# Pooled attention and routed experts: another order of the first loads, weight halves split earlier, two first-layer chunks in one group

## The chip, the core and the metric

The kernel runs on one core of one Trainium2 chip. The core has TensorE (matmuls, results in PSUM), VectorE, ScalarE, GpSimd and SyncE, each with an instruction stream of its own that runs in order; they wait for each other by semaphores. In profile rows they are PE (PEld for its weight loads), DVE, ACT, POOL and SP. The metric is the device time of the program in microseconds (us); lower is better.

## What is computed

Attention over keys and values that are averaged in groups of 8, then a layer of 8 experts of which each row takes one.

```python
k_p = k.reshape(B, H, Sp, pool, D).mean(axis=3)      # B=8, H=8, S=576, D=64, pool=8
v_p = v.reshape(B, H, Sp, pool, D).mean(axis=3)
scores = scale * np.matmul(q, k_p.transpose(0, 1, 3, 2))
attn = softmax(scores); x = attn @ v_p               # x: 4608 rows of 512
...
logits = x @ w_gate; e_idx = np.argmax(logits, axis=1)
gate_w = probs[np.arange(N), e_idx]; eom = sigmoid(x @ w_output_gate)
h = np.maximum(x[mask] @ w1[e], 0.0)                 # 512 -> 1024
out[mask] = gate_w[mask, None] * eom[mask, e, None] * (h @ w2[e])
```

Matmuls of the experts run on two-part operands: each f32 number is split into a high part (a rounded copy made by ScalarE) and a low part (what is left, a VectorE subtraction), and three products are summed.

## The kernel before

The attention works on 36 tiles of 128 rows (`NT`), a batch being 4.5 tiles. One pass of the main loop, `i` with halves `a` = 0, 1 (four heads each), issues: the scores of tile `i` (`scores`), the transposes of the probabilities of tile `i - 2` (`transpose_p`), the row maxima of tile `i` on VectorE (`peak`), the products with the values of tile `i - 3` (`values`), the exponentials on ScalarE (`softmax`) and the division (`normalise`). Two small generators' queues are worked between these (`work`): the routing of each group of four tiles and the pooling of values.

The order within each engine is written out by hand. What belongs to a batch is put into a table `plan` by `at(step, function, ...)`, and the entries of step `i + a/2 - 1/2` are issued at the end of pass (`i`, `a`), in the order in which they were put in: the batches' loads first, then their pooling, then the rest. For batch `b` with `f` = 4.5 `b`: keys are loaded at step `f - 8.5`, values at `f - 5` (not before step 0), queries at `f - 4.5`. All of these go through SP's one queue. Keys are pooled by three rounds of additions, on VectorE for batch 0 (`ready_k`) and on GpSimd (`pool_k`) later, then copied by ScalarE into `kbd` (`scale_k`). Values are pooled on VectorE for batch 0 (`first_v`); later GpSimd does the first round (`halve_v`, steps `f - 3` and `f - 2.5`) and VectorE the rest (`pool_v`, in the work queue from `f - 2`). All values pass through one buffer `vt`, so a load waits until the batch before has been pooled. Then seven ScalarE copies place them (`place_v`), TensorE turns them and multiplies them with the gates (`turn_v`, `gate_v`).

Towards the end of attention the first expert's weights are loaded in stages (`stage_in`) and split in halves of 512 columns (`split_hi` on ScalarE, `split_lo` on VectorE), and the first 384 rows of expert 0 are gathered and turned (`turn_x`). After the last tile the string `TAIL` gives the order: `M` one chunk of the first layer (12 matmuls of 384 columns, `hidden_chunk`), `H` and `L` its high and low part, `W` units of the routing, `a` and `d` halves of w1, `A` and `D` pieces of w2, `R` and `T` tables, `Y` a chunk of the second layer. Then the experts' loop runs; there GpSimd (`body` at line 1319) hands out the rows' ids and scales, gathers the next job's and scatters the results.

## Time and profile before

| what | us |
|---|---|
| median of three runs | 605.59 |
| lowest and highest of them | 602.8 and 607.97 |
| the profiled execution | 603.94 |
| its span, first to last instruction | 602.1 |

The profiled execution is one of its own and stands 1.65 us below the median. Its span begins at the first instruction, and the times in the rows below count from there. Attention lasts to about 151 us, the first layer and the start of the second of expert 0's first rows to about 183 us, and the experts' loop from there to the end. A row of the timeline gives start, length, engine, line and operation, what is written and read, the number of instructions merged, and in brackets how long the engine had been idle and for whom.

### The profile page before, as it was taken

Reading aid. Unit: us, or ns where it says so; the run is one execution under the profiler, and the core shown is the slowest. Engines: PE = TensorE matmul, PEld = TensorE weight load, DVE = VectorE, ACT = ScalarE, POOL = GpSimd, SP = SyncE. Lnnn points to the kernel's source line nnn. Section 1 sums busy time; section 2 is a strip of 40 time slices with the busy share of each in tenths; the row PEclk is TensorE's granted clock in tenths of the full one; section 3 lists DMA queues with packets and bytes.
Section 4 is the critical chain, followed back from the end, with each engine's and each line's share of the span. In section 5 each row is a group of like instructions: output and inputs, shape, how many; then the busy total and the mean of one; then the engine's idle time right before and its main releaser. Section 6 shows DMA issues by size and latency. Waiting matters only on the chain.

```text
span 602.1 us, 11826 instructions
## 1 busy us (share of the span) xinstructions
PE 572.3 (95%) x3427; PEld 519.2 (86%) x3428; DVE 365.1 (61%) x892; ACT 257.8 (43%) x709; POOL 223.1 (37%) x331
## 2 busy tenths in 40 slices
PE   2999999999899999999999999999999999999996
PEld 2898898888888989898989898898988898989894
DVE  6789999988888625698575323664263842232323
ACT  2988998787435304266344120441141420302120
POOL 2858789642524322233234131231202421213131
PEclk9999999999999999999999999999999999999999
DMA  9856899966377433589666213463033212010111
GB/s 337 312 236 270 316 349 369 348 232 198 140 238 182 170 99 118 147 234 335 177 215 201 62 37 88 139 195 65 35 139 102 46 21 84 2 52 19 41 30 36
DMA packets 44684, 96.61 MB, mean 160 GB/s; under 512 B 5515, under 2 KB 28475, under 8 KB 41664
## 3 DMA queue, kind: packets, MB, share of 16 engines
q1 hardware_dynamic: 29328, 48.95, 25.3%
q10 hardware_dynamic: 7488, 27.27, 13.5%
q0 software_dynamic: 7792, 19.61, 9.3%
q14 instruction: 57, 0.47, 0.3%
q8 instruction: 19, 0.31, 0.2%
HBM read 76.36 MB, written 22.91 MB: 165 GB/s over the span
## 4 chain that ended last, share of the span: by engine, by line
PE 68%; issue 2%; DVEq 0%; DVE 0%; POOL 0%; POOLq 0%
PE p_h L1015 34%; PE p_y L996 33%; PE p_y L665 1%; POOL out L1328 0%; DVE rows L1186 0%; DVEq L1189 0%; PE p_y L1050 0%; DVE q_even L1212 0%; DVEq L779 0%; DVEq L780 0%; DVEq L1219 0%; DVEq L910 0%; DVEq L837 0%; DVEq L1211 0%; DVEq L860 0%
## 5 line engine op out<-in xcount | busy, mean ns | idle before, releaser
L1095 ACT ACTIVATE ht<-p_h 128x384 fp32r<-128x384 f32 (+1 forms) x104 | 46.9, 451 | 245.9 <-PE p_h L1015 243.7
L1015 PE MATMUL p_h<-xt,w1b 128*128 128x384 f32 (+1 forms) x736 | 115.5, 317 | 1.9 <-issue 1.3
L1015 PEld LDWEIGHTS p_h<-xt,w1b 128*128 128x128 f32 x736 | 114.4, 189 | 3.2 <-issue 2.8
L1328 POOL DMA_INDIRECT out<-rows,dst x41 | 43.1, 1051 | 199.8 <-DVE rows L1186 196.6
L1197 DVE SCALAR_TENSOR_TENSOR ht<-p_h,ht 128x384 fp32r<-128x384 f32 (+1 forms) x104 | 52.3, 504 | 98.4 <-ACT ht L1095 98.3
L996 PE MATMUL p_y<-w2b,ht 128*128 128x512 f32 x480 | 110.4, 390 | 0.0
L996 PEld LDWEIGHTS p_y<-w2b,ht 128*128 128x128 f32 x480 | 89.8, 188 | 18.4
L1015 PE MATMUL p_h<-xt,w1a 128*128 128x256 f32 (+1 forms) x640 | 93.7, 306 | 1.2 <-DVE q_even L1212 1.0
L1015 PEld LDWEIGHTS p_h<-xt,w1a 128*128 128x128 f32 x640 | 92.8, 190 | 2.3 <-DVE q_even L1212 1.2
L996 PE MATMUL p_y<-w2a,ht 128*128 128x512 f32 x408 | 94.2, 390 | 0.4 <-PE p_y L665 0.4
L996 PEld LDWEIGHTS p_y<-w2a,ht 128*128 128x128 f32 x408 | 76.2, 188 | 16.4 <-issue 0.9
L1186 DVE TENSOR_SCALAR rows<-p_y,sc 128x512 f32<-128x512 f32 x41 | 30.1, 741 | 85.9 <-PE p_y L996 71.5
L287 ACT ACTIVATE p<-p_h,m 128x72 f32<-128x72 f32 x288 | 69.9, 345 | 13.4 <-DVE m L281 13.0
L309 PE MATMUL p_y<-vbd,pT 128*128 128x162 f32 (+3 forms) x400 | 68.5, 320 | 3.8 <-DVE xg L332 2.6
L1305 POOL DMA_INDIRECT rows<-xs,src x51 | 56.0, 1099 | 24.9 <-POOL src L1301 13.4
L309 PEld LDWEIGHTS p_y<-vbd,pT 128*128 128x128 f32 (+1 forms) x400 | 54.2, 179 | 8.7 <-issue 2.5
L440 POOL DMA_INDIRECT xs<-xg,where x36 | 36.1, 1003 | 42.5 <-DVE grec L326 20.7
L201 POOL TENSOR_TENSOR kq<-kq 128x288 f32<-128x288 f32 (+1 forms) x63 | 40.8, 673 | 15.0 <-DMA kq<-kT 14.2
L275 PE MATMUL p_h<-kbd,q_even 128*128 128x144 f32 (+1 forms) x160 | 28.9, 308 | 11.6 <-DMA q_even<-qT 8.8
L332 DVE TENSOR_TENSOR xg<-p_y,grec 128x240 f32<-128x240 f32 x72 | 35.3, 490 | 1.3
L1150 DVE STREAM_TRANSPOSE turned<-rows 128x512 f32<-128x512 f32 x51 | 32.4, 686 | 4.0 <-DMA rows<-xs 2.2
L275 PEld LDWEIGHTS p_h<-kbd,q_even 128*128 128x128 f32 (+1 forms) x160 | 22.9, 191 | 13.7 <-issue 9.3
(170 smaller groups left out, 660.3 us busy)
## 6 DMA issues: line engine op xcount, KB each, us to landing
stage<-wst ACTq DMA_DIRECT2D x52, 512.0 KB, 4.7
rows<-v SPq DMA_DIRECT2D x8, 1280.0 KB, 6.3
kq<-kT SPq DMA_DIRECT2D x7, 1152.0 KB, 12.0
rows<-xs SPq DMA_DIRECT2D x36, 192.0 KB, 3.8
stage<-wst SPq DMA_DIRECT2D x12, 512.0 KB, 6.0
kq<-qT SPq DMA_DIRECT2D x4, 1152.0 KB, 9.5
q_even<-qT SPq DMA_DIRECT2D x3, 1152.0 KB, 8.8
rows<-xs SPq DMA_DIRECT2D x20, 128.0 KB
```

The lines of the kernel that those rows point to most:

```text
L201: eng.tensor_tensor(k[:, :, 0:w], k[:, :, 0:w], k[:, :, w:2 * w], op=ALU.add)
L275: nc.tensor.matmul(s[r0:r0 + n, 144 * c:144 * c + 144], q_t[b][:, 2 * a + c, s0:s0 + n], kbd[b % 2][:, 2 * a + c, :], start=True, stop=True)
L287: nc.scalar.activation(pt[i % 3][:, o:o + KEYS], sv[:, h], AF.Exp, bias=m[:, h:h + 1])
L309: nc.tensor.matmul(av[r0:r0 + n, COLS * h:COLS * (h + n_heads)], pT[:, c, r0:r0 + n], vbd[b % 2][:, slot:slot + n_heads].rearrange("p h f ...
L332: nc.vector.tensor_tensor(xg[g][:, j, 0:LEAD + DM].rearrange("p (f h) -> p f h", h=H)[:, :, hs], avv[:, :, 0:GATE + D].rearrange("p h f -> ...
L440: ins = nc.gpsimd.indirect_dma_start(out=whole_rows(xs), out_offset=bass.IndirectOffsetOnAxis(ap=where, axis=0), in_=x.bitcast(I32), in_of ...
L996: i = mm(to, ht[:, h, f, P * k:P * k + P], w[:, part, o:o + DM], start=(f == 0 and part == 0 and h == 0), stop=(f == 7 and h == 1))
L1015: i = mm(to, w[:, part, o:o + P], x, start=(d == 0 and k == 0), stop=(d == 3 and k == len(terms) - 1))
L1095: act(ht[:, 0, f, 0:size * P], p_h[f % DEEP][:, 0:size * P], AF.Relu).then_inc(q["hh"], 1)
L1197: nc.vector.scalar_tensor_tensor(ht[:, 1, f, 0:n], src, 0.0, ht[:, 0, f, 0:n].bitcast(F32), op0=ALU.max, op1=ALU.subtract).then_inc(q["hl" ...
L1305: nc.gpsimd.indirect_dma_start(out=xm[:, k].bitcast(I32), out_offset=None, in_=xs, in_offset=bass.IndirectOffsetOnAxis(ap=src[:, k:k + 1], ...
L1328: nc.gpsimd.indirect_dma_start(out=out, out_offset=bass.IndirectOffsetOnAxis(ap=dst[:, k:k + 1], axis=0), in_=yb[2 if k == size - 1 else k ...
```

## The change

- The loads of batch 0 go in another order: half of the keys, the queries of tile 0, the other keys, the queries of tile 1, the values, the remaining queries. The host lays the queries of batch 0 out so that each of the three parts is contiguous in a partition, and `scores` reads them through `queries`.
- `first_v` of batch 0 moves from before the loop and step -0.5 to step 1, `turn_v` and `place_v` to 1.5. The values of batch 1 are loaded at step 1.5 in place of 0. `prepare_routing` moves from 1.5 to 4, and the transfer of empty rows from 3 to 5.
- All eight halves of the first expert's w1 are split in the attention, every 1.5 steps from step 25; before, four were, every 2.5 steps from 26, and four in the tail. `stage_in` begins at step 16 in place of 18.
- The first `M` of the tail does chunks 0 and 1 in one group, products with the high part of the rows first.
- In the experts' loop GpSimd waits for the scatters of a job at the head of the next one, and after the loop for the last ones; the bound of the scatter is kept in a register.

```diff
 
 
 
-TAIL = 'M W9 a H L W3 d M a H L W6 d M a H L W6 d M a H L W6 d A M H L W12 A D M H L A D R M H L A D T M D Y Y Y Y Y H L'.split()
+TAIL = 'M W9 H L W3 M A H L W6 D M A H L W6 D M A H L W6 D M A H L W12 D M H L R M H L T Y Y Y Y Y H L'.split()
 F0 = TAIL.count('Y')
 
 AHEAD = {3: 8, 2: 8, 1: 2}
...
 POS = (4, 6)
 BEHIND = 2
 TURN = 36.0
-AHEAD_OF_X = 4
+AHEAD_OF_X = 8
 
 
 class Shared:
...
     def load_v(b):
         nc.sync.dma_start(vt, v[b].rearrange("p (c f) -> p c f", c=5))
 
+    FIRST_Q = ((0, P), (P, P), (2 * P, S - 2 * P))
+
     def load_first():
         k_t[0], q_t[0] = sh.k[0], sh.q[0]
-        k, q = kT[0].rearrange("p (c r n) -> p c r n", r=POOL, c=4), qT[0].rearrange("p (c s) -> p c s", c=4)
+        k = kT[0].rearrange("p (c r n) -> p c r n", r=POOL, c=4)
+
+        def part_q(s, n):
+            nc.sync.dma_start(sh.q[0].rearrange("p c s -> p (c s)")[:, 4 * s:4 * s + 4 * n], qT[0][:, 4 * s:4 * s + 4 * n])
+
         nc.sync.dma_start(k_t[0][:, 0:2], k[:, 0:2])
+        part_q(*FIRST_Q[0])
+        nc.sync.dma_start(k_t[0][:, 2:4], k[:, 2:4])
+        part_q(*FIRST_Q[1])
         load_v(0)
-        nc.sync.dma_start(q_t[0][:, :, 0:P], q[:, :, 0:P])
-        nc.sync.dma_start(k_t[0][:, 2:4], k[:, 2:4])
-        nc.sync.dma_start(q_t[0][:, :, P:S], q[:, :, P:S])
+        part_q(*FIRST_Q[2])
+
+    def queries(b, c, s0, n):
+        if b:
+            return q_t[b][:, c, s0:s0 + n]
+        s, w = next(part for part in FIRST_Q if part[0] <= s0 < part[0] + part[1])
+        o = 4 * s + w * c + s0 - s
+        return q_t[0].rearrange("p c s -> p (c s)")[:, o:o + n]
 
     def pool_k(b, eng, w, c0, c1):
         k = k_t[b][:, c0:c1]
...
         s = s_t[i, a] = sh.p_h[(2 * i + a) % 3]
         for c in range(2):
             for r0, n, b, s0 in segments(i):
-                nc.tensor.matmul(s[r0:r0 + n, 144 * c:144 * c + 144], q_t[b][:, 2 * a + c, s0:s0 + n],
+                nc.tensor.matmul(s[r0:r0 + n, 144 * c:144 * c + 144], queries(b, 2 * a + c, s0, n),
                                  kbd[b % 2][:, 2 * a + c, :], start=True, stop=True)
 
     def peak(i, a):
...
         else:
             nc.vector.tensor_tensor(low, turned, high.bitcast(F32), op=ALU.subtract)
 
-    halves = list(range(AHEAD_OF_X, 8))
     layered, high, low, outputs, split_piece, split_done = [], [], [], [], [], [3, 2, 1, 0]
 
     def first_layer(kind):
         if kind == "M":
-            f = len(layered)
-            layered.append((sh.p_h + sh.p_y[1:])[f % 4][:, 0:WIDE * P])
-            hidden_chunk(nc, sh, f, layered[f], f == 0)
+            accs = {}
+            for _ in range(1 if layered else 2):
+                f = len(layered)
+                accs[f] = (sh.p_h + sh.p_y[1:])[f % 4][:, 0:WIDE * P]
+                layered.append(accs[f])
+            hidden_chunks(nc, sh, accs)
         elif kind == "Y":
             outputs.append(output_chunk(nc, sh, len(outputs), sh.p_y[0], 0))
-        elif kind == "a":
-            split_hi(halves[0])
-        elif kind == "d":
-            split_lo(halves.pop(0))
         elif kind == "A":
             split_piece.append(len(split_piece))
             split_hi(2 * 4 + split_piece[-1], 1)
...
     for b in range(1, B):
         f = S * b // P + 0.5 * (b % 2)
         at(f - 8.5, load_k, b)
-        at(max(f - 5, 0), load_v, b)
+        at(max(f - 5, 1.5), load_v, b)
         at(f - 4.5, load_q, b)
         for i, part in enumerate([(w, c, c + 1) for w in (4, 2) for c in range(4)] + [(1, 0, 4)]):
             step = f - 5.5 + 0.5 * (i // 2)
...
         at(f - 0.5, turn_v, b)
         at(f + 1.5, gate_v, b)
     for c in range(STAGES):
-        at(18 + 3 * c, stage_in, c)
+        at(16 + 3 * c, stage_in, c)
     for c in range(AHEAD_OF_X):
-        at(26 + 2.5 * c, split_hi, c)
-        at(27 + 2.5 * c, split_lo, c)
+        at(25 + 1.5 * c, split_hi, c)
+        at(25.5 + 1.5 * c, split_lo, c)
     for g in range(len(GROUPS)):
         at(sum(GROUPS[:g + 1]) + 2, lambda g: queue.append([route(g), 0, g]), g)
 
...
     prepare_buffers(2)
     prepare_counts()
     ready_k(0)
-    first_v(0)
     at(-0.5, ready_k, 1)
-    at(-0.5, first_v, 1)
-    at(1.5, prepare_routing)
-    at(3, no_rows, E)
+    for a in range(2):
+        at(1, first_v, a)
+    at(4, prepare_routing)
+    at(5, no_rows, E)
     for e in range(E):
         at(27 + e, no_rows, e)
     for c in range(3):
-        at(1, place_v, 0, c)
-    at(0.5, turn_v, 0)
+        at(1.5, place_v, 0, c)
+    at(1.5, turn_v, 0)
     at(2, gate_v, 0)
     for i in range(NT + 3):
         for a in range(2):
...
     return x.rearrange("p g f -> p (g f)"), x.rearrange("p g (d t) -> p d g t", d=4), halves
 
 
-def hidden_chunk(nc, sh, f, acc, late):
-    terms = [(d, part, x) for d in range(4) for part, x in ((0, 0), (0, 1), (1, 0))]
-    if late:
-        terms.sort(key=lambda term: term[2])
-    for d, part, x in terms:
+def hidden_chunks(nc, sh, accs):
+    terms = [(f, d, part, x) for f in accs for d in range(4) for part, x in ((0, 0), (0, 1), (1, 0))]
+    if 0 in accs:
+        terms.sort(key=lambda term: term[3])
+    seen = {f: 0 for f in accs}
+    for f, d, part, x in terms:
         o = DM * f + P * d
-        i = nc.tensor.matmul(acc, sh.w1[0][:, part, o:o + P], sh.xt[:, x, d, :], start=((d, part, x) == terms[0]), stop=((d, part, x) == terms[-1]))
-    return i
+        nc.tensor.matmul(accs[f], sh.w1[0][:, part, o:o + P], sh.xt[:, x, d, :], start=(seen[f] == 0), stop=(seen[f] == 11))
+        seen[f] += 1
 
 
 def output_chunk(nc, sh, f, acc, k):
...
             gather(X)
 
         def body(e, size, job, u, single, nth, more, last, late):
+            with eng.If(job > 0):
+                past("out", 16 * u)
             past("y", u + 1)
             copy(sc[:, 0:3:4 - size], nx[:, 0:size, 1]).then_inc(q["sc"], 1)
             copy(dst, nx[:, :, 0]).then_inc(q["c"], 1)
...
             for k in range(size):
                 past("y", u + k + 2)
                 nc.gpsimd.indirect_dma_start(out=out, out_offset=bass.IndirectOffsetOnAxis(ap=dst[:, k:k + 1], axis=0),
-                                             in_=yb[2 if k == size - 1 else k], in_offset=None, bounds_check=N - 1, oob_is_err=False).then_inc(q["out"], 16)
-            past("out", 16 * (u + size))
-
+                                             in_=yb[2 if k == size - 1 else k], in_offset=None, bounds_check=limit, oob_is_err=False).then_inc(q["out"], 16)
+
+        limit = eng.to_reg(N - 1)
         eng.nop().then_inc(q["on"], 1)
         rows = table(eng)
         with eng.If(rows[E + 1] > 2):
...
         job, slot = loops(eng, rows, body)
         for k in range(WIDE):
             past(f"x{k}", 16 * job + 16)
+        past("out", 16 * slot)
 
 
 def program():
...
     vs = np.zeros((B, P, 5, POOL * D), np.float32)
     for chunk, r0, head, k0, n in VROWS:
         vs[:, r0:r0 + n, chunk] = rows[:, head, k0:k0 + n]
+    qs = c(q.reshape(B, 4, 2, S, D).transpose(0, 2, 4, 1, 3)).reshape(B, P, 4 * S)
+    first = qs[0].reshape(P, 4, S)
+    qs[0] = np.concatenate([first[:, :, a:z].reshape(P, 4 * (z - a)) for a, z in ((0, P), (P, 2 * P), (2 * P, S))], axis=1)
     return {
-        "qT": c(q.reshape(B, 4, 2, S, D).transpose(0, 2, 4, 1, 3)).reshape(B, P, 4 * S),
+        "qT": qs,
         "kT": c(k.reshape(B, 4, 2, KEYS, POOL, D).transpose(0, 2, 5, 1, 4, 3)).reshape(B, P, 4 * POOL * KEYS),
         "v": vs.reshape(B, P, 5 * POOL * D),
         "wg": wg.reshape(P, 11 * GATE),
```

## Rows read from the trace of the kernel before

**Rows 1.** The page, busy time by engine

```profile
PE 572.3 (95%) x3427; PEld 519.2 (86%) x3428; DVE 365.1 (61%) x892; ACT 257.8 (43%) x709; POOL 223.1 (37%) x331
```

**Rows 2.** Windows: stretch, length, busy PE, PEld, DVE, ACT, POOL, clock, DMA share, GB/s

```profile
27.50:30.00 2.50, 2.50 (x23) 2.50 (x22) 2.11 (x7) 2.50 (x12) 2.50 (x5) 1.00 0.74 295
...
110.00:120.00 10.00, 8.72 (x60) 7.25 (x59) 9.90 (x34) 7.48 (x33) 6.13 (x11) 1.00 1.00 397
...
160.00:165.00 5.00, 5.00 (x31) 5.00 (x30) 4.72 (x28) 2.87 (x6) 3.39 (x3) 1.00 0.51 157
```

**Rows 3.** Timeline, first keys, scores and exponentials

```profile
4.64 1.60 DVE L201 TENSOR_TENSOR kq<-kq 128x576 f32<-128x576 f32 x3 [0.47 <-DMA kq<-kT]
...
6.33 0.65 ACT L206 ACTIVATE kbd<-kq 64x144 f32<-64x144 f32 x2 [4.05 <-DVE kq L201]
...
8.82 1.30 PE L275 MATMUL p_h<-kbd,q_even 128*128 128x144 f32 x4 [8.82 <-DMA q_even<-qT]
...
10.65 0.96 ACT L287 ACTIVATE p<-p_h,m 128x72 f32<-128x72 f32 x4 [3.67 <-DVE m L281]
...
12.86 2.29 PE L275 MATMUL p_h<-kbd,q_even 128*128 128x144 f32 x8 [2.73 <-ACT kbd L206]
```

**Rows 4.** Timeline, values of batches 0 and 1; DMA from 13 to 16 us

```profile
7.86 1.55 DVE L227 TENSOR_TENSOR rows<-rows 128x768 f32<-128x768 f32 x2 [1.62 <-DMA rows<-v]
...
13.21 0.29 DVE L227 TENSOR_TENSOR vp<-rows 128x128 f32<-128x128 f32 x1
...
13.53 0.33 SPq L188 DMA_DIRECT2D rows<-v  x1
...
14.44 0.38 SPq L181 DMA_DIRECT2D kq<-kT  x1
...
rows<-v SPq DMA_DIRECT2D x1, 1280.0 KB, 6.2
kq<-qT SPq DMA_DIRECT2D x1, 1152.0 KB, 9.1
kq<-kT SPq DMA_DIRECT2D x1, 1152.0 KB, 11.5
```

**Rows 5.** Timeline, pooling of batch 1 and the maximum ahead of it

```profile
15.59 5.72 POOL L201 TENSOR_TENSOR kq<-kq 128x288 f32<-128x288 f32 x9 [11.45 <-DMA kq<-kT]
...
21.28 3.79 POOL L223 TENSOR_TENSOR rows<-rows 128x256 f32<-128x256 f32 x5
...
21.93 0.46 DVE L281 TENSOR_REDUCE m<-p_h 128x4 f32<-128x288 f32 x1 [0.23 <-PE ptr L299]
...
23.41 1.07 DVE L227 TENSOR_TENSOR rows<-rows 128x384 f32<-128x384 f32 x1 [1.03 <-POOL rows L223]
...
40.07 0.54 DVE L227 TENSOR_TENSOR rows<-rows 128x384 f32<-128x384 f32 x1
```

**Rows 6.** Timeline, placing and turning the values of batch 0

```profile
16.50 0.40 ACT L249 ACTIVATE vT<-vtr 128x256 f32<-128x256 f32 x1
...
17.83 0.91 PE L256 MATMUL vg<-wgd,vT 128*128 128x64 f32 x6
...
17.90 1.28 ACT L238 ACTIVATE vbd<-vp,mask 128x128 f32<-128x128 f32 x4
...
19.07 0.82 ACT L241 ACTIVATE vbd<-vp,mask 128x64 f32<-128x64 f32 x3
```

**Rows 7.** Timeline, the first of the five routing constants

```profile
17.58 0.50 DVE L160 MEMSET stage<- 128x528 f32 x1
```

**Rows 8.** Groups by shape, 110 to 152 us: operation, count, busy us, mean ns

```profile
L472 DVE TENSOR_TENSOR w1a<-stage,w1a 128x512 fp32r<-128x512 f32 x4 | 2.9, 727 | 0.0
```

**Rows 9.** Timeline, TensorE's waits between attention and first layer

```profile
154.08 0.97 PE L659 MATMUL p_h<-xt,w1a 128*128 128x384 f32 x4 [0.61 <-DVE xt L483]
...
155.82 0.19 PE L372 MATMUL rk<-oh,tri 128*128 128x40 bf16 x1 [0.77 <-DVE oh L363]
```

**Rows 10.** Timeline, the last scatter

```profile
598.09 1.00 POOL L1328 DMA_INDIRECT out<-rows,dst  x1 [4.31 <-DVE rows L1186]
```

More of the change, by code (lines that the diff above doesn't have):

```diff
@@ L643, in attention_and_routing @@
             place_ids()
-    assert not halves and len(layered) == len(high) == len(low) == 8 and len(split_piece) == 4 and not split_done
+    assert len(layered) == len(high) == len(low) == 8 and len(split_piece) == 4 and not split_done
 def turned_rows(sh, k):
```

## The prediction

> **What bounds the kernel now.** I read the page first: TensorE is busy for 95% of the span, the next engine for 61% [rows 1]. So a change earns time only where TensorE stands still, or where it is made to stand still. The windows view tells where that is. From about 27 us on TensorE fills its windows (2.50 of 2.50 us, and 5.00 of 5.00 behind the attention), with small holes in the middle such as 8.72 of 10 us between 110 and 120, where VectorE has 9.90 [rows 2]. The granted clock is 1.00 in all of these rows, the 2.4 GHz level, so no term below is a clock term. What is left to win is the head, the seam between attention and first layer, and the few microseconds after the last matmul. The timeline of the head is therefore the view that matters: TensorE's first matmul starts at 8.82 us, held by the first queries, and the second group at 12.86 us, held by the second half of the keys [rows 3].
>
> **The new order of the first transfers.** Bytes and landings give the pace. Keys of half a batch have landed by 4.64 us, and all that stands in the queue up to the keys of batch 1 by 15.59 us [rows 3, 5]: 4248 KB (1280 values, 256 + 896 queries, 576 and 1152 keys, 88 gate weights) in 10.95 us, 388 KB per us. With the new order the queries of tile 0 (256 KB) are there at 5.3, the second keys at 6.8, the queries of tile 1 at 7.4, the values at 10.7, the rest at 12.6, and the keys of batch 1 at 15.6 as before, since the bytes ahead of them are the same.
>
> *First scores.* Pooling of the first keys ends at 4.64 + 1.60 = 6.24, ScalarE's copies by 6.98 [rows 3]; the queries are there, so scores start at 7.0 in place of 8.82 and end at 8.3 (1.30 for four). The maximum (0.46, [rows 5]) ends at 8.8; the second keys are pooled (1.60 again) by 10.4 and scaled (0.65) by 11.1. The next eight matmuls then start at 11.1 in place of 12.86: 1.8 us earlier. They end at 13.4 (2.29), the maxima of tile 1 at 13.9 and, after four more matmuls, 14.6.
>
> *Values of batch 0.* Their six additions on VectorE ran in its waiting times before, from 7.86 to 13.50, 3.3 us of work [rows 4]. Now they stand behind four maxima and start at 14.6, when VectorE has tile 2 to serve. Alone they would end at 17.9. But GpSimd pools the keys of batch 1 from 15.6 on, for 5.72 us [rows 5], and next to GpSimd an addition of 384 elements takes 1.07 us where it takes 0.54 without it [rows 5]. Taking about half of the remaining 2.3 us of additions as doubled and the rest as somewhat stretched, I add 1.9 us: 19.8.
>
> The Trainium skill, page "SBUF — State Buffer", section "Who interferes with whom", goes further: a VectorE instruction with two SBUF inputs against a GpSimd one that reads SBUF is not slowed but fully blocked until that one has ended. By that rule each of the five later additions could wait for a whole GpSimd instruction (5.72 / 9 = 0.64 us), 3.2 us in place of 1.9, and the sum below would be 1.3 us more. The 1.07 us row agrees with it (one wait of 0.53), and the sum goes by the row.
>
> *What is late next.* ScalarE waits for the maximum of tile 2, then does its exponentials (0.96, [rows 3]), then the seven copies that place the values (1.28 + 0.82), then the two copies of the turned values (0.40 for the larger, some 0.54 with the second) [rows 6]; TensorE's gate matmuls (0.91, [rows 6]) wait for these, and the scores of tile 3 stand behind them in TensorE's queue. From 19.8: maximum 20.3, exponentials 21.2, placed 23.3, turned 23.9, gate 24.8, then scores, two matmul groups and the second maximum of tile 3 at about 27.6. Without GpSimd in the way it is 25.7. Before, this maximum started at 21.93 and ended at 22.4 [rows 5].
>
> **Values of batch 1.** This is the part that decides. Their load was issued at 13.53, ahead of the queries of batch 1 and the keys of batch 2, and landed 6.2 us later, at 19.7; the keys, issued at 14.44, landed 11.5 us later, at 25.9, the queries between the two [rows 4]. Now the load sits at step 1.5, and SP's queue meets the queries (step 0) and the keys (step 0.5) first. The three pass one after the other, 3584 KB from 15.6 to 25.9, 348 KB per us; with no gap in front I take 388: queries 18.6, keys 21.5, values 24.8. GpSimd then halves them, 0.76 us each [rows 5], three for the first part: 27.1. VectorE already waited for that part before (1.03 us, until 23.41 [rows 5]), and every maximum stands behind it in order. So VectorE goes on at 27.1 by this chain, at 25.7 to 27.6 by the one above, where it went on at 23.41. **+3.8 us**, about the mean of 27.1 and 27.6 less 23.41 and less some lock waits that fall out; bounds +2.3 (25.7) and +5.5 (lock waits in full). TensorE was full from 27.5 on, so there is nothing behind that gives the time back.
>
> **Routing constants.** Five small VectorE instructions (0.50 us for the first, [rows 7], 1.55 in all) move from step 1.5 to 4, between maxima of tiles 4 and 5. Nearest row is their own: 0 if hidden in VectorE's spare time there (2.11 of 2.50 [rows 2]), 1.55 if not. I take **+0.3**. The transfer of empty rows that follows them is off every path.
>
> **Four more halves split in attention.** Four copies on ScalarE and four subtractions on VectorE, 0.73 us each by the row of the attention [rows 8], come into tiles 25 to 36. Cover: VectorE is at 9.90 of 10 around 115 us but freer later, and the last one stands ahead of the turning of the gathered rows. 0 if TensorE stays the bound, 2.9 if VectorE is. **+0.7**, near the lower end because the row of 110 to 120 is the fullest one. The earlier weight transfers of the stages cost nothing: the queue has room behind the last keys.
>
> **Two chunks joined.** In the seam TensorE waits 0.61 us for the low part of the rows and 0.77 us for the routing's one-hot [rows 9]. With 16 high-part matmuls ahead of the first low-part one, and 24 ahead of the ranks, both waits are covered: -1.4. A late subtraction in front takes some back: **-1.2**, bounds -1.4 and -0.4. The splits that leave the first layer's stage free VectorE and ScalarE there, but TensorE has 5.00 of 5.00 in that stage [rows 2], so this earns nothing.
>
> **GpSimd's wait and limit.** The wait for the last scatter moves into the next job's head: the same number, one branch later. The maxima of VectorE and TensorE do not hang on it. At the end 3.0 us pass from the last scatter's end at 599.09 to the span's end at 602.1 [rows 10]; now the loop's exit and three waits run while the rows land. **-0.4**; bounds 0 and -0.8.
>
> **Sum.** The profiled execution took 603.94 us (602.1 of span and 1.8 around it). 603.94 + 3.8 + 0.3 + 0.7 - 1.2 - 0.4 = 607.1. The median of the three runs lies 1.65 us above this execution, which the range has to cover.
>
> **Rivals.** *A, the head gains.* The scores do start 1.8 us earlier; if the values of batch 1 are not late in effect (they land before 22 because the queue serves them together with the others, and VectorE's additions fit between the maxima), all behind moves up by this. For it: the 1.8 us are sure as far as the second scores. Against: the three came one after the other, 6 us from the first to the third. It decides if the first halving ends before 23.4. Time: 603.94 - 1.8 + 0.7 - 1.2 - 0.4 = 601.2. *B, the head comes out even*: the later stall of VectorE is worked off in the holes that TensorE has in the middle of the attention (1.28 us between 110 and 120 [rows 2], and a few like it). For it: those holes are there; against: VectorE makes them, and it has more to do now. 603.94 + 0 + 0.3 + 0.7 - 1.2 - 0.4 = 603.3. *C, VectorE binds*: the lock waits in full and the splits at half their price, 607.1 + 1.3 + 0.8 = 609.2. For it: 9.90 of 10; against: the row behind is freer.
>
> **Chances.** Forecast 0.5 (its own range 605 to 609), A 0.2, B 0.18, C 0.12. The range from 600.0 to 611.0 takes in A and C and the spread of the three runs at each side. A measurement of this kernel tells about 1% (6 us) from no change. Faster by over 1% would need A and 3 us more: 0.05. Slower by over 1% needs C and 2 us more, or the upper bounds of several terms: 0.08. Within 1%: 0.87.
>
> **What would show it.** In the timeline of the changed kernel: first scores near 7.0 and the second near 11.1; the load of the values of batch 1 landing near 24.8; VectorE idle ahead of its addition for batch 1, released by GpSimd, until about 27; TensorE full only from about 31. In the seam no wait for the low part and none for the one-hot. The prediction is wrong if the values of batch 1 land near 20, if VectorE passes their addition before 24, or if TensorE's holes between 110 and 150 shrink.

## The result, and the profile after

The changed kernel takes 610.28 us (median of 15 executions, 608.1 to 612.5) against 605.75 us for the kernel before (15 executions, 602.8 to 608.5): ratio 1.0079, 95% interval 1.0062 to 1.0096. That is a loss of 4.5 us. It is less than the 1% that the prediction called the limit of a measurement, but the interval lies above 1. A ratio in this document leaves out executions more than 1.5% above the fastest of their kernel, so it need not equal the quotient of the medians beside it. The profiled execution took 609.97 us, 6.0 us more than the one of before (603.94), which stood low among its runs.

The page's busy times and its line of granted clocks in 40 slices (tenths of full speed):

```profile
PE 576.3 (95%) x3427; PEld 522.8 (86%) x3428; DVE 367.1 (60%) x892; ACT 257.7 (42%) x709; POOL 222.6 (37%) x331
...
PEclk9699999999999999999999999999999999999999
```

The counts of TensorE and VectorE are those of [rows 1], but TensorE is busy 4.0 us longer with the same matmuls, and the second slice has a 6. The windows show where. Columns as in [rows 2]; the column before the last two is the granted clock:

```profile
15.00:17.50 2.50, 0.71 (x5) 0.47 (x4) 2.43 (x5) 1.24 (x6) 1.26 (x2) 1.00 1.00 424
17.50:20.00 2.50, 0.26 (x1) 0.07 (x1) 2.43 (x3) 0.00 (x0) 2.50 (x3) 0.74 0.98 417
20.00:22.50 2.50, 2.14 (x9) 1.85 (x9) 1.06 (x3) 1.79 (x8) 2.42 (x6) 0.50 0.56 153
22.50:25.00 2.50, 1.30 (x6) 1.04 (x5) 0.07 (x1) 2.50 (x12) 0.37 (x1) 0.50 0.95 392
25.00:27.50 2.50, 2.50 (x10) 2.40 (x11) 0.99 (x5) 1.16 (x4) 1.66 (x3) 0.50 0.01 4
27.50:30.00 2.50, 2.50 (x15) 2.48 (x14) 1.32 (x4) 1.58 (x7) 2.50 (x5) 0.71 0.00 0
30.00:32.50 2.50, 2.50 (x25) 1.83 (x24) 2.40 (x5) 1.25 (x6) 2.50 (x4) 1.00 0.00 0
```

TensorE does 0.97 us of work in the five microseconds from 15 to 20, its clock falls from 1.00 to 0.50 (2.4 to 1.2 GHz), and it is back at 1.00 only in the window from 30. From 25 to 27.5 TensorE looks full, with 10 instructions in a window where e3 below, at a clock of 1.00, has 21. The timeline of the same stretch:

```profile
7.20 1.30 PE L289 MATMUL p_h<-kbd,q_even 128*128 128x144 f32 x4 [7.20 <-ACT kbd L220]
...
11.24 4.19 PE L289 MATMUL p_h<-kbd,q_even 128*128 128x144 f32 x16 [2.73 <-ACT kbd L220]
...
14.97 1.54 DVE L241 TENSOR_TENSOR rows<-rows 128x768 f32<-128x768 f32 x2
...
16.24 6.63 POOL L215 TENSOR_TENSOR kq<-kq 128x288 f32<-128x288 f32 x9 [12.09 <-DMA kq<-kT]
...
19.54 0.76 DVE L241 TENSOR_TENSOR vp<-rows 128x128 f32<-128x128 f32 x1
20.23 0.45 DVE L295 TENSOR_REDUCE m<-p_h 128x4 f32<-128x288 f32 x1
20.33 0.33 SPq L188 DMA_DIRECT2D rows<-v  x1
...
23.85 1.70 PE L270 MATMUL vg<-wgd,vT 128*128 128x64 f32 x6 [1.20 <-ACT vT L263]
...
25.48 1.33 PE L289 MATMUL p_h<-kbd,q_even 128*128 128x144 f32 x4
...
25.84 3.46 POOL L237 TENSOR_TENSOR rows<-rows 128x256 f32<-128x256 f32 x5 [2.98 <-DVE vbd L272]
...
29.27 0.46 DVE L295 TENSOR_REDUCE m<-p_h 128x4 f32<-128x288 f32 x1 [0.30 <-PE ptr L313]
...
29.65 0.97 DVE L241 TENSOR_TENSOR rows<-rows 128x384 f32<-128x384 f32 x1
```

Read it downwards. The scores come earlier by 1.6 us each (8.82 and 12.86 in [rows 3]). The six additions for the values of batch 0 run from 14.97 to 20.30 on VectorE, next to GpSimd from 16.24 on. The maximum of tile 2 (20.23) waits behind them, and so does the whole chain. The gate matmuls take 1.70 us where [rows 6] has 0.91. VectorE's first addition for batch 1 starts at 29.65, where [rows 5] has 23.41.

To follow the loss through the attention I use one instruction per tile, the first division of the tile's output on VectorE. For tile 19 it is this row, first of the kernel before, then after:

```profile
92.44 0.41 DVE L332 TENSOR_TENSOR xg<-p_y,grec 128x240 f32<-128x240 f32 x1
```

```profile
99.36 0.41 DVE L346 TENSOR_TENSOR xg<-p_y,grec 128x240 f32<-128x240 f32 x1
```

The difference, 6.92 us, stands between 6.7 and 6.9 in every tile from 3 to 26 (tiles are counted from 0): the head makes it, and nothing gives it back. At tile 28 it grows to 7.36 and at tile 34 to 7.95. The seam between attention and first layer then takes back 1.8, the last microseconds 0.9, by these rows of after:

```profile
159.75 4.46 PE L672 MATMUL p_h<-xt,w1a 128*128 128x384 f32 x24 [0.20 <-ACT xt L495]
...
164.05 0.20 PE L386 MATMUL rk<-oh,tri 128*128 128x40 bf16 x1
...
181.37 2.97 PE L678 MATMUL p_y<-w2a,ht 128*128 128x512 f32 x12 [0.99 <-PEq L1409]
...
603.43 0.75 DVE L1199 TENSOR_SCALAR rows<-p_y,sc 128x512 f32<-128x512 f32 x1 [4.60 <-PE p_y L1009]
```

(PEq is TensorE's sequencer.) The first layer starts 7.96 us later than before (151.79 there). The two waits of [rows 9] are gone: 24 matmuls run without a break and the ranks at 164.05 follow without a wait. The second layer resumes at 181.37, 6.14 later than before (175.23). The last scaling starts at 603.43, 6.98 later (596.45), and from there to the span's end it is 4.77 us against 5.65. In all: +6.9 (head), +1.05 (attention from tile 28), -1.8 (seam), +0.8 (experts' loop), -0.9 (end) make 6.05, the difference of the spans being 6.1.

The +0.8 in the experts' loop is largely one wait of TensorE for VectorE at an expert with a single tile of rows, 1.65 us here and 1.03 before. In the ten kernels below, whose code at this place differs in GpSimd's wait alone, it is between 0.3 and 1.9 us and goes with no edit. I take it as scatter between executions.

### The profile page after: what moved, and what is told of

The parts are those of the page before. It is cut to its first block, busy times and chain, and to the rows that moved or that the text cites. A ratio compares the mean times of both kernels' runs of the same rounds, so it can differ in the third digit from the quotient of the medians.

```text
span 608.2 us, 11863 instructions
## 1 busy us (share of the span) xinstructions
PE 576.3 (95%) x3427; PEld 522.8 (86%) x3428; DVE 367.1 (60%) x892; ACT 257.7 (42%) x709; POOL 222.6 (37%) x331
## 4 chain that ended last, share of the span: by engine, by line
PE 66%; issue 2%; DVE 1%; DVEq 1%; ACT 0%; POOL 0%; POOLq 0%
PE p_h L1028 33%; PE p_y L1009 31%; PE p_y L678 1%; ACT w2b L1097 0%; DVE q_even L1225 0%; POOL out L1343 0%; DVE rows L1199 0%; DVE ht L1210 0%; DVE xt L1159 0%; DVEq L1202 0%; DVEq L1158 0%; ACT ht L1116 0%; DVEq L792 0%; DVEq L793 0%; DVE w2b L1187 0%
## 5 line engine op out<-in xcount | busy, mean ns | idle before, releaser
L215 POOL TENSOR_TENSOR kq<-kq 128x288 f32<-128x288 f32 (+1 forms) x63 | 42.5, 700 | 15.4 <-DMA kq<-kT 14.6
L289 PE MATMUL p_h<-kbd,q_even 128*128 128x144 f32 (+1 forms) x160 | 30.8, 325 | 9.9 <-ACT kbd L220 9.9
L295 DVE TENSOR_REDUCE m<-p_h 128x4 f32<-128x288 f32 x72 | 32.3, 449 | 8.4 <-PE p_h L289 7.8
L289 PEld LDWEIGHTS p_h<-kbd,q_even 128*128 128x128 f32 (+1 forms) x160 | 24.9, 207 | 11.8 <-issue 7.4
```

The source lines that it names most:

```text
L215: eng.tensor_tensor(k[:, :, 0:w], k[:, :, 0:w], k[:, :, w:2 * w], op=ALU.add)
L289: nc.tensor.matmul(s[r0:r0 + n, 144 * c:144 * c + 144], queries(b, 2 * a + c, s0, n), kbd[b % 2][:, 2 * a + c, :], start=True, stop=True)
```

## Experiments: which part of the head costs

My theory was the prediction's: the values of batch 0, summed behind the maxima of tile 1, delay what stands behind them. The rivals: the transfers' new order is what costs; or the loss comes from other parts and the head only shows it. Four kernels undo one part or do it alone. The shift of the first division against the kernel before, worked out from the timelines of all kernels of this document as for tile 19 above, in us:

| kernel | tile 7 | tile 19 | tile 35 |
|---|---|---|---|
| after | 6.74 | 6.92 | 7.96 |
| e1, old head | 0.44 | 0.94 | 3.75 |
| e2, new head alone | 7.68 | 7.47 | 9.47 |
| e5, new transfers, values early | 0.57 | 0.40 | 3.29 |
| e6, old transfers, values late | 8.01 | 7.73 | 12.85 |
| e3, matmuls in the gap | 6.91 | 6.32 | 9.13 |
| e4, queries before keys of batch 1 | 5.42 | 6.04 | 8.80 |
| e9, and keys of batch 2 later | 4.67 | 4.90 | 7.76 |
| e7, and matmuls in the first gap | 4.94 | 4.40 | 9.01 |
| e10, and in the second gap | 3.58 | 3.41 | 13.34 |
| e8, joined chunks and GpSimd's wait alone | -0.04 | -0.23 | 2.69 |

Tiles 7 to 19 show the head. Each row is one execution. The two with the head of before (e1, e8) differ by 0.5 us at tile 7 and 1.2 at tile 19, the two with the new head (after, e2) by 0.94 and 0.55, so a difference under 1 us between two rows says little. Between tiles 19 and 27 some of these executions jump by up to 10 us; that is another matter, told in the last section.

**e1: the changed kernel with the old head.** The loads, their layout and the steps of the head as before; splits, joined chunks and GpSimd's wait as after.

```diff
         nc.sync.dma_start(k_t[0][:, 0:2], k[:, 0:2])
-        part_q(*FIRST_Q[0])
-        nc.sync.dma_start(k_t[0][:, 2:4], k[:, 2:4])
-        part_q(*FIRST_Q[1])
         load_v(0)
-        part_q(*FIRST_Q[2])
+        nc.sync.dma_start(q_t[0][:, :, 0:P], q[:, :, 0:P])
+        nc.sync.dma_start(k_t[0][:, 2:4], k[:, 2:4])
+        nc.sync.dma_start(q_t[0][:, :, P:S], q[:, :, P:S])
...
-        at(max(f - 5, 1.5), load_v, b)
+        at(max(f - 5, 0), load_v, b)
...
     ready_k(0)
+    first_v(0)
     at(-0.5, ready_k, 1)
-    for a in range(2):
-        at(1, first_v, a)
-    at(4, prepare_routing)
-    at(5, no_rows, E)
+    at(-0.5, first_v, 1)
+    at(1.5, prepare_routing)
+    at(3, no_rows, E)
...
-        at(1.5, place_v, 0, c)
-    at(1.5, turn_v, 0)
+        at(1, place_v, 0, c)
+    at(0.5, turn_v, 0)
```

> The changed kernel with the head of before: transfers, values, placing, routing constants and the load of the second batch's values at their old places; the earlier splits, the joined chunks and GpSimd's moved wait stay. Theory (all of the loss is made in the head, by 30 us): the divisions of tiles 1 to 27 fall within 0.2 us of those of before, the seam is 1 us later by the splits, some 0.8 us is ahead of before after the joined chunks, the end 0.9 us shorter; time about 604, ratio to before 0.997. Rival (the earlier splits cost as much as the head): ratio 1.002 or more.

Measured: 604.33 us, ratio 0.9984 (0.9954 to 1.0015). The loss is gone, and tile 7 is 0.44 late.

**e2: the kernel before with the new head.** The reverse edit.

> The kernel before with the head of the changed one alone. Theory: tiles 1 to 27 are 6.9 us later than before, and this shift lasts to the end; about 612, ratio 1.010 to 1.012, slower than the whole change. Rival (half of the loss is made later, by splits and tail): ratio 1.005 or less.

Measured: 612.52 us, ratio 1.0106 (1.0068 to 1.0144). Tile 7 is 7.68 late, 0.94 more than in after with the same head; its granted clock is 0.73 in the window from 30 to 32.5 us, where after has 1.00. The two together settle that the head makes the loss. That the rest gives a little back, the times do not settle: the interval of e1 takes in 1, and that of e2 overlaps that of after.

**e5: the new transfers, the values early again.** The scores may start at 7.2 us, but the additions go ahead of the maxima of tile 1.

```diff
-    for a in range(2):
-        at(1, first_v, a)
+    at(-0.5, first_v, 0)
+    at(0, first_v, 1)
-    at(4, prepare_routing)
-    at(5, no_rows, E)
+    at(1.5, prepare_routing)
+    at(3, no_rows, E)
...
-        at(max(f - 5, 1.5), load_v, b)
+        at(max(f - 5, 0.5), load_v, b)
...
-        at(1.5, place_v, 0, c)
-    at(1.5, turn_v, 0)
+        at(1, place_v, 0, c)
+    at(0.5, turn_v, 0)
```

> The changed kernel with its new transfers, but the first values summed early: the first part behind the pooling of the second keys, the second part at step 0, and the load of batch 1's values, the turning, placing and routing constants at early steps again. Theory (the place of the additions makes the loss, not the order of the transfers): the additions end by about 15.5 us, before GpSimd pools keys; tiles 1 to 9 are 0 to 1 us later than in the kernel before, and the time is that of the kernel with the old head, about 604.5. Rival (the order of the transfers makes the loss): 3 us or more stay.

Measured: 605.33 us, ratio 0.9987 (0.9952 to 1.0022). The timeline of its head:

```profile
7.35 1.30 PE L289 MATMUL p_h<-kbd,q_even 128*128 128x144 f32 x4 [7.35 <-ACT kbd L220]
...
10.73 1.55 DVE L241 TENSOR_TENSOR rows<-rows 128x768 f32<-128x768 f32 x2
...
19.04 0.90 PE L270 MATMUL vg<-wgd,vT 128*128 128x64 f32 x6
...
23.43 1.07 DVE L241 TENSOR_TENSOR rows<-rows 128x384 f32<-128x384 f32 x1 [0.74 <-POOL rows L237]
```

The gate matmuls run at 19.04 in 0.90 us, and VectorE passes its addition for batch 1 at 23.43, 0.02 us from where it was before. So the early scores cost nothing, and they bring nothing: the addition waits 0.74 us for GpSimd, as it waited 1.03 before.

**e6: the old transfers, the values late.** The other corner.

> The changed kernel with the transfers and the layout of before; the values of batch 0 are still summed behind two tiles' maxima. Theory: scores start 1.6 us later and all six additions run beside GpSimd; tiles 1 to 9 are about 8.4 us later than before, about 611.7, 1.5 us over the changed kernel. Rival (the order of the transfers makes the loss): 3 us or more of the 6.9 are gone.

Measured: 613.39 us, ratio 1.0087 (1.0065 to 1.011); tile 7 is 8.01 late. With e5 this makes a square of four. Values late costs 6.2 us at tile 7 with the new transfers (6.74 against 0.57) and 7.6 with the old ones (8.01 against 0.44). The transfers' order changes the shift by 0.1 with the values early and by -1.3 with them late. So the late values are the cause, and the order of the transfers is not. "Late" stands here for everything that e5 moves together: the six additions, the placing and turning that need them, the load of batch 1's values and the routing constants. The square does not part these; the constants are worth at most 0.2 (below), and the load cannot be issued before the additions have read its buffer.

## Experiments: what makes the late place so dear

The prediction had +3.8 for the head, and it was +6.9. Candidates: the low clock; GpSimd beside the additions; the load of the values of batch 1.

**e3: matmuls in TensorE's gap.** 28 f32 products (56 records) that keep TensorE at work from 15.6 to 22.6 us, all else as after.

```diff
+    def filler():
+        for k in range(28):
+            nc.tensor.matmul(sh.p_y[1][:, 0:144], ident, kbd[0][:, k % 4, :], start=True, stop=True)
...
+    at(1.5, filler)
     at(1.5, turn_v, 0)
```

> The changed kernel with 28 extra matmuls of 144 columns on TensorE ahead of the turning of the first values, where it stood idle from 15.7 to 20.4 us; their result is overwritten. Clock theory: the granted clock stays at 1.00 where it was 0.50 from 18.5 to 28.5 us, the gate matmuls take 0.91 us in place of 1.70, and VectorE's first addition for batch 1 moves from 29.65 to about 28, where GpSimd's halving then ends last; 1.5 us less than the changed kernel, about 608.8. Rival (the load of batch 1's values bounds, the clock is harmless): the addition stays within 0.3 us of 29.65.

Measured: 610.55 us, ratio 1.007 (1.0046 to 1.0093). Windows, then timeline:

```profile
22.50:25.00 2.50, 2.26 (x19) 1.90 (x16) 0.46 (x1) 2.50 (x12) 0.10 (x1) 1.00 0.92 385
25.00:27.50 2.50, 2.50 (x21) 2.50 (x21) 1.93 (x8) 2.44 (x10) 0.00 (x0) 1.00 0.12 43
```

```profile
24.03 1.01 PE L274 MATMUL vg<-wgd,vT 128*128 128x64 f32 x6 [0.24 <-ACT vT L263]
...
27.09 0.46 DVE L299 TENSOR_REDUCE m<-p_h 128x4 f32<-128x288 f32 x1
...
27.64 3.77 POOL L237 TENSOR_TENSOR rows<-rows 128x256 f32<-128x256 f32 x5 [5.04 <-DVE m L299]
...
29.77 1.07 DVE L241 TENSOR_TENSOR rows<-rows 128x384 f32<-128x384 f32 x1 [2.22 <-POOL rows L237]
```

The clock stays at 1.00 in these windows and the compute chain shrinks. From the start of the gate matmuls to the start of the second maximum of tile 3 it is 3.06 us (24.03 to 27.09), where after has 5.42 (23.85 to 29.27): the clock costs this chain 2.4 us. But the addition does not come near 28, where it was expected, and the shift hardly moves, because VectorE now waits 2.22 us for GpSimd's halving, which starts 5.04 us after GpSimd's last work, once the load issued at 20.51 has landed. That load took longer than in after, whose issue at 20.33 is nearly the same. From issue to landing, first in after, then in e3:

```profile
rows<-v SPq DMA_DIRECT2D x1, 1280.0 KB, 5.4
```

```profile
rows<-v SPq DMA_DIRECT2D x1, 1280.0 KB, 7.0
```

So it landed at 25.7 in after and at 27.5 here. Three of the five halvings free VectorE's addition: in after they end at 27.9, 1.7 us ahead of the addition at 29.65, and here at 29.7, just ahead of it. The load of the values of batch 1 is a second bound behind the half clock, and in this one execution it took the place of the first. Why it landed later is not shown, so e3 says what the clock costs the chain, 2.4 us, and not what it costs the kernel.

**e4: the queries of batch 1 before its keys.** The queue serves 1152 KB of queries first, so GpSimd's pooling of the keys starts later and leaves VectorE's additions alone.

```diff
-        at(f - 4.5, load_q, b)
+        at(f - 4.5 if b > 1 else -4.5, load_q, b)
```

> The changed kernel with the queries of batch 1 loaded ahead of its keys, so that GpSimd begins to pool these keys about 3 us later (19.3 in place of 16.24) and does not run beside VectorE's additions for the first values. Theory of the shared port: the six additions take about 3.4 us in place of 5.3 and end at 18.3 in place of 20.3; everything behind moves up by about 2 us, so about 608.3. Rival (the additions are slow for another reason): they still end near 20.3 and the time is that of the changed kernel or more.

Measured: 609.38 us, ratio 1.0058 (1.0037 to 1.008). Its timeline:

```profile
14.93 1.54 DVE L241 TENSOR_TENSOR rows<-rows 128x768 f32<-128x768 f32 x2
...
17.96 0.29 DVE L241 TENSOR_TENSOR vp<-rows 128x128 f32<-128x128 f32 x1
18.09 5.72 POOL L215 TENSOR_TENSOR kq<-kq 128x288 f32<-128x288 f32 x9 [13.95 <-DMA kq<-kT]
...
28.23 1.06 DVE L241 TENSOR_TENSOR rows<-rows 128x384 f32<-128x384 f32 x1 [0.44 <-POOL rows L237]
```

The six additions take 3.32 us (14.93 to 18.25) where they took 5.33 beside GpSimd, and GpSimd's nine take 5.72 where they took 6.63: the neighbourhood cost 2.0 us on one side and 0.9 on the other. The Trainium skill, page "SBUF — State Buffer", section "Who interferes with whom", read as the prediction reads it, would have each of the five later additions wait for a whole GpSimd instruction, 3.2 us by the prediction's working; these additions show 2.0, near the 1.9 that went into the sum. The shift falls by only 1.3 (tile 7) or 0.9 (tile 19) where about 2 was expected, and VectorE then waits 0.44 us for the halving again.

**e9: e4, and the keys of batch 2 behind the values of batch 1.** So that this load has the queue to itself.

```diff
-        at(f - 8.5, load_k, b)
+        at(f - 8.5 if b != 2 else 2, load_k, b)
```

> The kernel of the fourth experiment (queries of batch 1 ahead of its keys) with the keys of batch 2 loaded behind the values of batch 1. The values of batch 1 then land near 23 and GpSimd halves them right behind the keys, so that VectorE does not wait for it; the rest of the head is not touched and TensorE is still at a granted clock of 0.50. Expected by the clock theory: VectorE's addition for batch 1 at 27.8 in place of 28.23, tiles 1 to 9 about 5.0 us later than before.

Measured: 610.45 us, ratio 1.0052 (1.0034 to 1.007). VectorE's addition for batch 1 comes at 27.59 without a wait, tile 7 is 4.67 late. The compute chain alone is left, and it is still at half speed:

```profile
21.68 1.71 PE L270 MATMUL vg<-wgd,vT 128*128 128x64 f32 x6 [1.21 <-ACT vT L263]
...
27.59 0.55 DVE L241 TENSOR_TENSOR rows<-rows 128x384 f32<-128x384 f32 x1
```

The clock is printed as 1.00 in this stretch of this trace, while the gate matmuls take 1.71 us, as in after and e7 at a printed 0.50 and not as in e10 at 1.00 (0.90). I go by the matmuls. The profiled execution is also the fastest of the seven (607.62 us).

**e7: e9, and eleven products in the gap behind the scores.**

```diff
+    def filler():
+        for k in range(11):
+            nc.tensor.matmul(sh.p_y[1][:, 0:144], ident, kbd[0][:, k % 4, :], start=True, stop=True)
...
+    at(1.5, filler)
     at(1.5, turn_v, 0)
```

> The kernel of the run with the keys of batch 2 behind, and in addition 11 extra matmuls of 144 columns where TensorE stands idle from 15.5 to 18.3 us; their result is overwritten. Clock theory: granted clock 1.00 throughout; gate matmuls 0.9 us, scores 0.7; VectorE's addition for batch 1 near 26.0, tiles 1 to 9 about 3.3 us later than before, 1.7 us less than without the extra matmuls. Rival (the clock is harmless): no difference between the two.

Measured: 610.13 us, ratio 1.0036 (1.0018 to 1.0054). The expectation failed, as the clock fell all the same.

```profile
21.72 1.71 PE L274 MATMUL vg<-wgd,vT 128*128 128x64 f32 x6 [2.23 <-ACT vT L263]
```

TensorE had a second gap, 2.23 us ahead of the gate matmuls; the window from 20 to 22.5 has a clock of 0.70, that from 22.5 a clock of 0.50. Tile 7 is 4.94 late, tile 19 4.40, about as in e9. This run says nothing on what the clock costs.

**e10: e7, and nine more products in the second gap.**

```diff
+    at(2, filler, 9)
     at(2, gate_v, 0)
```

> The kernel with queries of batch 1 ahead of its keys, keys of batch 2 behind its values, and extra matmuls (results overwritten) in both gaps of TensorE: 11 ahead of the turning and 9 ahead of the gate matmuls, where the run with 11 alone still stood idle for 2.2 us and had its clock lowered. Clock theory: granted clock 1.00 to 30 us, gate matmuls 0.9 us in place of 1.71; VectorE's addition for batch 1 near 26.2, where GpSimd's halving ends, in place of 27.6; tiles 1 to 9 about 3.4 us later than before in place of 4.8. Rival (the clock is harmless): 4.8 stays.

Measured: 612.75 us on a chip where before took 609.3, ratio 1.004 (1.0003 to 1.0077). The profiled execution took 619.75 us and lost 10 us after tile 19, so only its head is read here:

```profile
22.50:25.00 2.50, 2.50 (x21) 2.38 (x20) 1.12 (x6) 1.15 (x5) 2.42 (x6) 1.00 1.01 418
```

```profile
22.47 0.90 PE L274 MATMUL vg<-wgd,vT 128*128 128x64 f32 x6
...
26.43 1.07 DVE L241 TENSOR_TENSOR rows<-rows 128x384 f32<-128x384 f32 x1 [0.55 <-POOL rows L237]
```

At full clock the gate matmuls take 0.90 us although they start 0.8 later than in e9, VectorE's addition comes 1.2 earlier, and tile 7 is 3.58 late, tile 19 3.41, where e9 has 4.67 and 4.90. By these two executions the low clock costs the head 1.1 to 1.5 us once the other two bounds are out of the way. The times of the whole kernels are too coarse to show it: the interval of e10 takes in the whole of e9's.

So, taken away in this order and read from one execution each, the head's 6.9 us divide like this: some 2.0 for GpSimd beside the additions and the load that comes next (after to e9, 6.92 to 4.90 at tile 19), some 1.1 to 1.5 for the clock (e9 to e10), and about 3.4 that stay with the late place alone, since only moving the additions back (e5) removes them. In another order the shares would differ, since the bounds hide one another.

## Experiment: the seam

The prediction priced the joined chunks at -1.2 and said that the splits which leave the tail earn nothing there. Theory: the joining alone takes away the two waits, 1.4 us. Rival: the joining gains only if the splits leave the tail.

**e8: the kernel before with joined chunks and GpSimd's wait, the splits left in the tail.**

```diff
-TAIL = 'M W9 a H L W3 d M a H L W6 d M a H L W6 d M a H L W6 d A M H L W12 A D M H L A D R M H L A D T M D Y Y Y Y Y H L'.split()
+TAIL = 'M W9 a H L W3 d M a H L W6 d M a H L W6 d M a H L W6 d A M H L W12 A D M H L A D R M H L A D T D Y Y Y Y Y H L'.split()
...
+            accs = {}
+            for _ in range(1 if layered else 2):
...
+            hidden_chunks(nc, sh, accs)
...
+            with eng.If(job > 0):
+                past("out", 16 * u)
...
-            past("out", 16 * (u + size))
...
+        past("out", 16 * slot)
```

> The kernel before with only the joined chunks and GpSimd's moved wait of the change; head, splits and their places as before. Theory (these two are the parts that gain): no wait of TensorE for the low part and the one-hot at the seam, 1.4 us, and an end 0.9 us shorter: 2.3 us less than before, ratio 0.996. Rival (the joined chunks need the earlier splits): a wait for a late half appears in the tail and the ratio is 0.998 or more.

Measured: 607.7 us against 609.3 for before on that chip, ratio 0.9999 (0.9963 to 1.0036). The first layer starts at 154.47 and the second layer resumes at 177.87, 2.68 and 2.64 later than before: no gain in the seam. Its timeline shows where the 1.4 us of removed waits went:

```profile
174.06 2.35 DVE L472 TENSOR_TENSOR w2a<-stage,w2a 128x1024 fp32r<-128x1024 f32 x2
...
175.33 0.73 PE L669 MATMUL p_y<-w2a,ht 128*128 128x512 f32 x2 [0.68 <-DVE w2a L472]
...
177.87 4.34 PE L669 MATMUL p_y<-w2a,ht 128*128 128x512 f32 x18 [1.81 <-PEq L1400]
```

TensorE is ahead and runs into VectorE, which still splits a piece of w2: 0.68 us of waiting there, and 1.81 at the exit to the experts' loop where before and after have 0.99. Together 1.5; what makes the exit longer was not followed. The rival holds: the joining without the earlier splits earns nothing here, and with them it earns 1.8 with either head (from the start of the first layer to the exit before takes 23.4 us, e8 23.4, after 21.6, e1 21.6). The splits without the joining were not run. The end, from the last scaling to the span's end, is 4.8 us here too, as in every kernel with GpSimd's new wait, and 5.6 in e2, which has the old one.

No version was found that beats the kernel before by more than the measurement's uncertainty; e1 (0.9984) and e5 (0.9987) come nearest, and both intervals reach past 1.

## Why the prediction was right, and where its steps failed

The forecast was 607.1, between 600 and 611, within 1% of before; the median is 610.28. The direction and the range held, and so did the mechanism in outline: the scores come earlier, the values of batch 0 are summed late, VectorE reaches its addition for batch 1 late, and nothing behind gives the time back. Which of the two chains binds and how long it is, the forecast had wrong. The size shows it: a loss of 6.0 us between the profiled executions, the basis of the sum, where 3.2 was forecast. The median lies outside the forecast's own 605 to 609 and nearer to rival C's 609.2; the wide range, made for the rivals and the spread, is what held. There is luck in it too: the head was 3.1 us worse than forecast, and the seam and the end together 1.1 us better for reasons that were in part not foreseen.

- **First scores.** Forecast 7.0 and 11.1, measured 7.20 and 11.24. Right, to 0.2 us.
- **Additions beside GpSimd.** Forecast to end at 19.8, measured 20.3. The 1.9 us for the neighbourhood was 2.0 (e4).
- **The chain behind them.** Forecast 27.6 for the end of the second maximum of tile 3, measured 29.73 (29.27 + 0.46). This is the step that failed. Up to the gate matmuls it holds: 23.9 forecast, 23.85 measured. From there it gave 3.7 us, and after took 5.88 us; e3 at full clock took 3.52 (24.03 to 27.55). The sentence "no term below is a clock term" was wrong. The gap that the forecast itself put ahead of the gate matmuls was never asked what it does to the clock, though the trace of before shows one operation at two speeds: four score matmuls take 1.30 us at 8.82, after the idle start [rows 3], and 0.76 at 21.06, and after takes 1.33 for four at 25.48 with a granted clock of 0.50. The windows of before print 1.00 at 8.82 as well, so only the durations could have told:

```profile
21.06 0.76 PE L275 MATMUL p_h<-kbd,q_even 128*128 128x144 f32 x4
```

The forecast's first scores used the slow figure, its chain behind the gap the fast ones.
- **Values of batch 1.** Forecast to land at 24.8 and to bind at 27.1. They were issued at 20.33 and landed 5.4 us later, at 25.7. The reason given, the queue ahead of them, was not the one: the issue waited for the single buffer until the late additions had read it (20.30), and SP's queue stood still for 8.7 us for that. And the load, called the part that decides, did not bind in after, where the addition at 29.65 has no wait for GpSimd; it stood 1.7 us behind the other chain, and bound in e3. The prediction's sign in the timeline, "VectorE idle ahead of its addition for batch 1, released by GpSimd", was not seen.
- **The head's term.** +3.8 with bounds of +2.3 and +5.5; measured +6.9. The bounds took the lock waits in, but no clock. Adding the 2.2 us of the clock to the mean of the two chains gives 6.0, to the slower chain alone 27.6 + 2.2 - 23.41 = 6.4; what makes up the last half microsecond behind the addition was not separated. Without the neighbourhood and at full clock the chain was forecast at +2.3; e10, with neither the neighbourhood nor the low clock, still has +3.4, with 0.55 of waiting for the halving in it.
- **Routing constants.** Forecast +0.3. The shift is constant from tile 3 to 26, so at most 0.2 can be theirs.
- **Splits in attention.** Forecast +0.7, measured +1.05 (0.46 at tile 28, 0.6 at tile 34), inside the bounds.
- **Joined chunks.** Forecast -1.2 with -1.4 as the far bound; measured -1.8. Both waits went as said. The excess comes from the splits that left the tail, of which the prediction said that they earn nothing: e8 shows the pair at work. TensorE at 5.00 of 5.00 us in one window did not mean that VectorE is free of deadlines at the end of the stage.
- **GpSimd's wait.** Forecast -0.4, measured -0.9 (5.65 to 4.77 from the last scaling to the end). From the last scatter's end to the span's end 3.0 us became 2.2, which is the lower bound of -0.8; the remaining 0.1 lies between scaling and scatter. That the wait now runs wholly while the rows land is the reading, not a measurement.
- **Rivals.** A (head gains) fails in after, whose first halving starts at 25.84 and so cannot end before 23.4; and even with the values early and the early scores kept (e5) the addition for batch 1 still comes at 23.43. B (head even) is refuted by the shift that stays at 6.9 from tile 3 to 26: the holes of TensorE did not take anything back. C (VectorE binds) fits the size but not the cause.

## What to carry to other kernels

Work that moves behind a chain's first link is paid with the chain's whole length, so follow it to the next transfer's issue, to the buffer that it frees, and to the matmuls at its end; and wherever a forecast itself makes TensorE idle, price the matmuls behind the gap at both rates that the trace shows for them. When one bound is taken away and the time stays, look for the second one at the same place before calling the first innocent. Removing a wait of the bounding engine paid here only where the engine that feeds it later in the same stage got room too.

## What the runs showed of the hardware that I had not expected

A small subtraction on VectorE, 128x32 elements with both inputs in SBUF, takes 0.19 us in the last groups of every run, where GpSimd has no keys left to pool. In the routing of one group it meets GpSimd's pooling of keys. From the kernel before, then e1, then e2:

```profile
110.18 1.70 DVE L354 TENSOR_TENSOR d<-lg,mx 128x32 f32<-128x32 f32 x1
```

```profile
111.71 3.81 DVE L354 TENSOR_TENSOR d<-lg,mx 128x32 f32<-128x32 f32 x1
...
112.61 4.18 POOL L201 TENSOR_TENSOR kq<-kq 128x288 f32<-128x288 f32 x7
...
115.89 0.82 PE L309 MATMUL p_y<-vbd,pT 128*128 128x162 f32 x4 [2.89 <-DVE xg L332]
```

```profile
117.66 4.42 DVE L368 TENSOR_TENSOR d<-lg,mx 128x32 f32<-128x32 f32 x1
...
122.45 0.82 PE L323 MATMUL p_y<-vbd,pT 128*128 128x162 f32 x4 [2.90 <-DVE xg L346]
```

It took 1.70, 3.81 and 4.42 us, and TensorE waited 2.9 us behind it in the last two. GpSimd's longest instructions there take 0.8 us each, so this is not a wait for one of them: VectorE's instruction lasts while GpSimd goes through several, and in e1 and e2 it ends within 0.1 us of the end of one. The Trainium skill, page "SBUF — State Buffer", section "Who interferes with whom", says that a VectorE instruction with two SBUF inputs contends with a GpSimd one that reads SBUF, and calls the lock on the shared port pair exclusive; the contention agrees. That the wait ends with one GpSimd instruction, as the prediction read the page, does not. In after the same subtraction took 1.10 us, in e10 an addition at another place 5.08. In e2 the granted clock fell after TensorE's wait (0.70 in the window from 122.5, 0.62 in that from 125). The jumps near tile 20, in e9 and others, come together with another long routing instruction, the comparison behind the subtraction, which took 1.72 us there. Such a meeting depends on where the two streams happen to stand, moves the rest of the attention by 1 to 4 us (10 in e10), and so makes an edit in the head look like a loss around tile 24. It may also be a part of the spread of the kernel before (602.8 to 608.5), which was not tested.
